# Strassen's algorithm for the output product of a fused attention and gated-layer chain, with its weight tiles and late sources arranged anew

## The chip, the cores and the metric

One core of a Trainium2 chip. The metric is the device time of one execution in microseconds; runs of this kernel differ by a few tenths of a microsecond.

## The reference, cut to what matters

```python
# attention (not touched): p attends k, v; q attends the result
x = attn_out.transpose(0, 2, 1, 3).reshape(B * S, H * D)   # 4608 x 512
# first layer (not touched): w_in 512 x 2048, w_out 2048 x 512
h = x @ w_in
x = (h * sigmoid(h)) @ w_out                               # 4608 x 512
# second layer: w1, w2 512 x 1024, w3 1024 x 1024, w_out 1024 x 512
a = x @ w1
b = x @ w2
h = a * b @ w3
return h @ w_out                                           # 4608 x 512
```

All in fp32.

## The kernel before

Each fp32 operand of a large matmul is split into a high part (rounded to the format of TensorE's fast fp32 mode) and a low part (the rest), and three matmuls add high x high, low x high and high x low. The high part is a ScalarE copy, the low part a subtraction on VectorE or GpSimd (`split_hi` L82, `split_lo` L91, `mm3` L98 to L100). Matmuls take 128x128 stationary tiles.

*First stage* (up to about 865 us). Attention and the first layer run over `items`, (batch, half, 128 rows of d_ff): `ps_h` products, a gate (`sg`, `gg`), its parts (`gh`, `gl`), `ps_x` products. The rows x are stored to `x2_d` in DRAM. In the last batches, `prepare_second` (L950) prepares the second layer's weights between these items. It decodes w1, w2, w3 and w_out; it multiplies w3 by w_out (`product`, L1012), so that one 1024x512 matrix remains, in eight tiles of 128 rows, whose split parts go to `w34_d`; and for half of w1 and w2 it forms the seven left factors of Strassen's algorithm (`left_factors` L935, parts `w12s`), which go to `w12_d`. The steps of `left_factors` wait in a list, `later`, from which `some(2)` takes two at a time. The decoded sources of the other half are stored to `late_d`. Six items before the stage's end (`prep_end`, L1064) the pool `early` opens, the first 768 tokens (`x2r`), two units of left factors and the first two weight tiles are loaded, and `first_right_factors` (L1113) makes the right factors of these tokens (tiles `xcb..`, `xct..`).

*Second stage*. The 4608 tokens are six groups g of 768 (GT), d_ff of the second layer four pairs mp of 128-row tiles: 24 items (g, mp). `emit_ab` (L1280) computes a = x w1 and b = x w2 of an item, one in each pass over x = 0, 1, by Strassen's algorithm in Winograd's form: seven products of 6 matmuls with 384 moving columns (W) in four PSUM banks `b1` to `b4`, in the order a11 b11, s1 t1, s2 t2, a22 t4, a12 b21, s3 t3, s4 b22, with sums on VectorE (L1286) and copies on ScalarE between them. Its weights are a unit (1.8 MB) in four buffers, `wunits`; `load_unit` (L1162) refills a buffer when its pass is over. In the second pass, `gate` (L1301) multiplies a by b and splits the result into `abh`, `abl`. `emit_o` (L1360), called for the item before within the first pass, is the plain output product: six tiles of 128 tokens, for each six matmuls of 512 columns (two weight tiles `w34`, three parts) into one of four banks `ps_o`. In the first item of a group ScalarE copies the result to the accumulator `oacc[t]`, in the others VectorE adds it (L1373), and the last stores it.

While the first two items run, `last_left_factors` (L1180) makes the left factors of w1's and w2's other half: for each of four pieces it loads two sources from `late_d` into `zl`, makes sums and parts (each step behind one product of `emit_ab`, three at a time) and writes each part to `w12_d`; low parts are all on GpSimd. Units 4 and 5 may be loaded only when 22 and 44 of these steps are out. Within each group, the rows of the next group are loaded (`load_x2`, L1088, after the first item), `right_sums` (L1139, GpSimd) forms its sums, and in the last item's second pass `right_factors` (L1153) splits them, alternately with GpSimd and VectorE for the low parts.

All DMAs of the second stage are issued by SP's queue in order. Each engine executes its own instructions in a fixed order, which a planner sets when the program is built: it orders by a modelled time, and among ready instructions by the order in the source. Matmuls of `ps_o` and `ps_ab` therefore stand mixed in the trace, and a load can stand ahead of its place in the source.

## Time and profile before

| | |
|---|---|
| median of 3 runs | 1457.34 us (1457.23 to 1457.74) |
| profiled execution | 1457.94 us, of which the span (first to last instruction) 1455.70 us |
| TensorE matmuls / weight loads busy | 1388.5 us (95%) / 1298.9 us (89%), 8540 each |
| VectorE, ScalarE, GpSimd busy | 959.4 us (66%), 685.3 us (47%), 684.9 us (47%) |
| mean granted TensorE clock | 0.986 of full speed |

Times are us from the span's start. PE is TensorE, PEld its weight loads, DVE VectorE, ACT ScalarE, POOL GpSimd, SP the engine that issues most DMAs. Matmuls are pipelined, so the distance of two starts, and not the length of a row, is what one costs. A line number can be that of a helper (L82, L91, L98 to L100); the tile names tell what is computed. "<-" in a group is output from inputs; behind a wait it names what ended it.

### The profile page before, as it was taken

How to read it: one execution, taken by the hardware profiler on the slowest of the kernel's cores; microseconds unless marked ns; L12 is line 12 of the kernel's file. 1: busy time of each engine (PE TensorE's matmuls, PEld its weight loads, DVE VectorE, ACT ScalarE, POOL GpSimd, SP SyncE). 2: the span in 40 equal slices, each digit the busy share in tenths (PEclk: the TensorE clock that was granted, in tenths of full speed). 3: DMA queues.
4: the chain of work that ended last, by engine and by line, in shares of the span. 5: the costliest groups of instructions: out<-in, count | busy, mean ns of one | idle time of the engine just before them, and what ended most of it. 6: DMA issues, size and time to landing. Idle time of an engine off the chain costs nothing.

```text
span 1455.7 us, 24332 instructions
## 1 busy us (share of the span) xinstructions
PE 1388.5 (95%) x8540; PEld 1298.9 (89%) x8540; DVE 959.4 (66%) x1812; ACT 685.3 (47%) x1531; POOL 684.9 (47%) x666
## 2 busy tenths in 40 slices
PE   7799899999999999999999999599999999999998
PEld 5588799899999999999998998499999989899897
DVE  5897866569776588667499746365574565645646
ACT  6866555555665556654465544132233322332321
POOL 3768755856879657686676525222040120310100
PEclk9899999999999999999999999799999999999999
DMA  8597545845567444562567578946464464554521
GB/s 317 187 308 251 167 142 169 262 135 152 160 199 227 145 134 141 174 178 79 184 218 237 197 289 298 359 153 239 152 226 165 158 233 184 197 211 152 196 102 44
DMA packets 147802, 281.04 MB, mean 193 GB/s; under 512 B 14560, under 2 KB 98784, under 8 KB 141536
## 3 DMA queue, kind: packets, MB, share of 16 engines
q1 hardware_dynamic: 137184, 266.91, 54.9%
q10 hardware_dynamic: 10496, 12.59, 2.4%
q8 instruction: 67, 1.10, 0.3%
q14 instruction: 55, 0.45, 0.1%
HBM read 213.12 MB, written 66.32 MB: 192 GB/s over the span
## 4 chain that ended last, share of the span: by engine, by line
PE 72%; DVE 9%; DMA 7%; issue 5%; ACT 4%; POOL 2%; SPq 1%; ACTq 0%; DVEq 0%; POOLq 0%
PE ps_ab L1272 22%; PE ps_x L98 6%; PE ps_x L99 6%; PE ps_x L100 6%; PE ps_o L98 5%; PE ps_o L99 5%; PE ps_o L100 5%; PE ps_h L98 3%; PE ps_h L100 3%; PE ps_h L99 3%; DMA m_d<-ms 1%; DMA unit<-w_d 1%; DVE gg L846 1%; DMA mr<-m_d 1%; PE ps_w L98 1%
## 5 line engine op out<-in xcount | busy, mean ns | idle before, releaser
L98 PE MATMUL ps_x<-gh,wo 128*128 128x288 f32 x1024 | 301.1, 297 | 2.2 <-DVE xs L883 0.6
L99 PE MATMUL ps_x<-gh,wo 128*128 128x288 f32 x1024 | 300.2, 296 | 0.0
L100 PE MATMUL ps_x<-gl,wo 128*128 128x288 f32 x1024 | 288.9, 297 | 1.5 <-POOL gl L91 1.4
L91 POOL TENSOR_TENSOR gl<-gg,gh 128x288 fp32r<-128x288 f32 x256 | 227.6, 891 | 102.0 <-ACT gh L82 83.0
L1272 PE MATMUL ps_ab<-xct,unit 128*128 128x384 f32 x1152 | 231.1, 340 | 4.0 <-DVE r L1286 4.0
L1272 PEld LDWEIGHTS ps_ab<-xct,unit 128*128 128x128 f32 x1152 | 206.4, 190 | 9.7 <-DVE r L1286 6.6
L98 PEld LDWEIGHTS ps_x<-gh,wo 128*128 128x128 f32 x1024 | 192.4, 188 | 5.6 <-DVE xs L883 2.0
L1272 PE MATMUL ps_ab<-xcb,unit 128*128 128x384 f32 x864 | 179.3, 340 | 16.1 <-DMA unit<-w_d 16.1
L99 PEld LDWEIGHTS ps_x<-gh,wo 128*128 128x128 f32 x1024 | 192.6, 188 | 2.1 <-issue 1.2
L82 ACT ACTIVATE gh<-gg 128x288 fp32r<-128x288 f32 x256 | 112.7, 443 | 167.7 <-DVE gg L846 160.1
L100 PEld LDWEIGHTS ps_x<-gl,wo 128*128 128x128 f32 x1024 | 188.1, 189 | 3.7 <-POOL gl L91 2.8
L91 POOL TENSOR_TENSOR mq<-mr,mq 128x256 fp32r<-128x256 f32 x168 | 137.4, 818 | 109.7 <-DVE mq L86 53.8
L846 DVE SCALAR_TENSOR_TENSOR gg<-sg,ps_h 128x288 f32<-128x288 f32 x256 | 114.5, 447 | 104.6 <-ACT sg L841 51.7
L91 POOL TENSOR_TENSOR xcb<-x2r,xcb 128x768 fp32r<-128x768 f32 x15 | 32.5, 2183 | 308.7 <-ACT xcb L82 308.7
L98 PE MATMUL ps_h<-a,mq 128*128 128x288 f32 x512 | 156.1, 305 | 20.4 <-DVE gg L846 16.2
L1272 PEld LDWEIGHTS ps_ab<-xcb,unit 128*128 128x128 f32 x864 | 155.6, 190 | 22.2 <-issue 11.8
L99 PE MATMUL ps_h<-a,mq 128*128 128x288 f32 x512 | 152.1, 297 | 0.0
L100 PE MATMUL ps_h<-a,mq 128*128 128x288 f32 x512 | 151.7, 296 | 0.0
L841 ACT ACTIVATE sg<-ps_h 128x288 f32<-128x288 f32 x256 | 103.4, 405 | 82.3 <-PE ps_h L100 52.0
L1286 DVE TENSOR_TENSOR r<-p,ps_ab 128x384 f32<-128x384 f32 x96 | 52.8, 550 | 129.7 <-PE ps_ab L1272 129.6
L82 ACT ACTIVATE p<-ps_ab 128x384 f32<-128x384 f32 x96 | 47.1, 492 | 176.0 <-PE ps_ab L1272 99.9
L98 PEld LDWEIGHTS ps_h<-a,mq 128*128 128x128 f32 x512 | 96.7, 189 | 28.6 <-DVE gg L846 21.3
(182 smaller groups left out, 2874.6 us busy)
## 6 DMA issues: line engine op xcount, KB each, us to landing
unit<-w_d SPq DMA_DIRECT2D x48, 1792.0 KB, 6.7
mr<-m_d SPq DMA_DIRECT2D x144, 128.0 KB, 2.6
raw<-in_moe_w_dram SPq DMA_DIRECT2D x32, 512.0 KB, 4.1
wz<-wi_d SPq DMA_DIRECT2D x48, 256.0 KB, 3.8
m_d<-ms SPq DMA_DIRECT2D x96, 128.0 KB, 3.0
x_d<-xs SPq DMA_DIRECT2D x20, 576.0 KB, 3.6
raw<-in_moe_w_out_dram SPq DMA_DIRECT2D x22, 512.0 KB, 4.1
out_dram<-ob SPq DMA_DIRECT2D x36, 256.0 KB, 4.9
```

The costliest lines, as they stand in the source:

```text
L82: A.activation(out=dst, in_=src, func=ACTF.Copy, scale=mul)
L91: (eng or V).tensor_tensor(out=lo, in0=src, in1=hi.bitcast(F32), op=ALU.subtract)
L98: T.matmul(out=dst, lhsT=wh, rhs=xh, start=start, stop=False)
L99: T.matmul(out=dst, lhsT=wl, rhs=xh, start=False, stop=False)
L100: return T.matmul(out=dst, lhsT=wh, rhs=xl, start=False, stop=stop)
L841: ins = A.activation(out=sg, in_=ps, func=ACTF.Tanh, scale=0.5)
L846: ins = V.scalar_tensor_tensor(out=gg, in0=sg, scalar=1.0, in1=ps, op0=ALU.add, op1=ALU.mult)
L1272: T.matmul(out=bank, lhsT=w[:, kt, LEFT[left], wp], rhs=xt[:, kt, xp], start=first and (kt, n) == (0, 0), stop=last and (kt, n) == (1, 2), ...
L1286: V.tensor_tensor(out=dst, in0=p, in1=q, op=op)
```

## The change

The output product too is computed by Strassen's algorithm. For each item the gated 768 tokens x 256 features are a 2x2 block matrix (a11 .. a22) with four sums s1 .. s4, all split into `lf` parts in `left_part`; the pair of weight tiles is a 2x2 block matrix (b11 .. b22) with four differences t1 .. t4. Seven products of nine matmuls (256 columns, three token tiles, three parts) go to chains of PSUM tiles of two banks, two of them at a time (`ps_o`, bufs 2, before 4 of one bank); the partial sums after each product are added to five accumulators of 768 columns in SBUF. After a group's last item GpSimd (VectorE at the very end) adds accumulator 3 to 5 and subtracts 4 from it. The seven steps stand as single steps between the products of the next item's `emit_ab`.

The weight factors of the first two pairs are made in `prepare_second` and stored in split form (`w34f_d`), by ScalarE's queue; the other two pairs stay whole in `w34_d` and are made in the second stage (`last_right_steps`), behind the late left factors. The sources of the first two late pieces are loaded at `prep_end`, into a ring of four `tmp` slots that also holds all sums. The late left factors go through one buffer with four writes for each piece, and part of their low parts go to VectorE. There are three unit buffers instead of four. `load_x2` moves behind a group's third item.

```diff
@@ prepare_second
+    def right_steps(z, sums, part):
+        b11, b12, b21, b22 = z
+        t1, t2, t3, t4 = (sums[:, i] for i in range(4))
...
+        return [
+            lambda: part("b11", b11), lambda: sub_(t1, b12, b11), lambda: part("t1", t1),
+            lambda: sub_(t2, b22, t1), lambda: part("t2", t2), lambda: sub_(t3, b22, b12),
+            lambda: part("b22", b22), lambda: sub_(t4, t2, b21), lambda: part("t3", t3),
+            lambda: part("b21", b21), lambda: part("t4", t4),
+        ]
...
-                    t = dp.tile([128, 2, 512], F32R, tag="w34s", name="w34s")
-                    split(t[:, 0], t[:, 1], ps_w)
-                    move(out=w34_d[i], in_=t)
+                    t = dp.tile([128, 512], F32, tag="w34s", name="w34s", bufs=5)
+                    act_copy(t, ps_w)
+                    z34[i] = t
+                    if i >= KM2 // 2:
+                        store(out=w34_d[i], in_=t, age=0)
+                    elif i > 1:
...
+                        def part(name, src):
+                            t = dp.tile([128, 2, 256], F32R, tag="w12s", name="w12s", bufs=4)
+                            split(t[:, 0], t[:, 1], src)
+                            store(out=w34f_d[mp][:, SECOND[name]], in_=t, age=0)
+
+                        later.extend(right_steps(z, sums, part))
...
-                        some(2)
+                        some(3)
@@ second stage, weights
+    def spare_tmp(k, n):
+        t = early.tile([128, 1024], F32, tag="tmp", name="tmp", bufs=4)
+        return t[:, 0:k * n].rearrange("p (k n) -> p k n", k=k)
...
+    def last_right_steps(mp):
+        w34[mp] = mid.tile([128, 7, 2, 256], F32R, tag=f"w34_{mp}", name=f"w34_{mp}")
+        t = spare_tmp(2, 512)
+        for y, m in enumerate(pair(mp)):
+            move(out=t[:, y], in_=w34_d[m])
+        sums = spare_tmp(4, 256)
+        def part(name, src):
+            d = w34[mp][:, SECOND[name]]
+            split(d[:, 0], d[:, 1], src, eng=G if name[0] == "b" else V)
...
@@ last_left_factors
-        z = load(0)
         for n in range(4):
             x, kt = divmod(n, 2)
-            sums = low.tile([128, 4, 256], F32, tag="suml", name="suml")
+            sums = spare_tmp(4, 256)
+            both = mid.tile([128, 2, 7, 2, 128], F32R, tag="w34_3", name="w12l")
             def part(j, src):
-                t = low.tile([128, 2, 2, 128], F32R, tag="w12s", name="w12s", bufs=7)
-                split(t[:, :, 0], t[:, :, 1], src.rearrange("p (j n) -> p j n", j=2), eng=G)
-                move(out=w12_d[:, 2:4, x, kt, j], in_=t)
+                t = both[:, :, j]
+                split(t[:, :, 0], t[:, :, 1], src.rearrange("p (j n) -> p j n", j=2), eng=G if j < 4 else V)
+                for js in {3: [slice(0, 4)], 6: [slice(4, 7)]}.get(j, []):
+                    for half in range(2):
+                        move(out=w12_d[:, 2 + half, x, kt, js], in_=both[:, half, js])
...
@@ at prep_end
-            for _ in range(2):
-                room_unit(early)
-                load_unit()
+            room_unit(early)
+            load_unit()
             load_w34(early, 0)
+            for n in range(2):
+                load_zl(n)
@@ emit_ab
+        before = o_steps(i - 1) if i else []
+        at_once = () if final else (2, 4, 6, 7, 8, 10, 11)
...
+        def left_part(name, src, eng=None):
...
+                c = mid.tile([128, 2, W], F32R, tag=f"lf{name}", name="lf")
+            split(c[:, 0], c[:, 1], src, eng=eng)
+            parts[name] = c
...
             def step():
+                if place[0] in at_once and before:
+                    before.pop(0)()
+                place[0] += 1
...
-                gate(m1, 0)
+                a11 = gate(0, 0)
+                left_part("a11", a11)
...
+                a12 = gate(1, 0)
+                a22 = gate(1, 1)
+                left_part("a12", a12, G)
+                left_part("a22", a22, G)
...
+                a21 = gate(0, 1)
+                s12, s34 = (spare_tmp(2, W) for _ in range(2))
+                add(s12[:, 0], a21, a22)
+                left_part("s1", s12[:, 0])
+                add(s12[:, 1], s12[:, 0], a11, ALU.subtract)
+                left_part("s2", s12[:, 1])
+                add(s34[:, 1], a12, s12[:, 1], ALU.subtract)
+                left_part("s4", s34[:, 1], G)
+                add(s34[:, 0], a11, a21, ALU.subtract)
+                left_part("s3", s34[:, 0], G)
@@ o_steps, in place of emit_o
+        def sum_up(k, ps):
+            if k not in oacc:
+                oacc[k] = low.tile([128, 3, 256], F32, tag=f"o{k}", name="ob")
+                act_copy(oacc[k], ps)
+            else:
+                V.tensor_tensor(out=oacc[k], in0=oacc[k], in1=ps, op=ALU.add)
...
+        def run(chain_, left, right, fresh, done, k):
+            if fresh:
+                banks[chain_] = ps_o.tile([128, 1024], F32, tag="o", name="ps_o")[:, 0:768]
+            ps = banks[chain_].rearrange("p (t n) -> p t n", t=3)
+            for t in range(3):
+                l = parts[left][:, :, 128 * t:128 * t + 128]
+                w = w34[mp][:, SECOND[right]]
+                for n, (lp, wp) in enumerate(((0, 0), (1, 0), (0, 1))):
+                    T.matmul(
+                        out=ps[:, t], lhsT=l[:, lp], rhs=w[:, wp], start=fresh and t != 1 and n == 0,
+                        stop=done and t != 0 and n == 2, skip_group_check=True,
+                    )
+            sum_up(k, ps)
...
+            run("a", "a11", "b11", True, False, 1)
+            run("b", "s1", "t1", True, False, 5)  
+            run("a", "s2", "t2", False, False, 2) 
+            run("b", "s4", "b22", False, True, 2) 
+            run("a", "s3", "t3", False, True, 3)  
+            run("c", "a12", "b21", True, True, 1) 
+            run("d", "a22", "t4", True, True, 4)  
@@ the loop over items2
-        if mp == 0 and g + 1 < NG:
-            with tc.issue_after(behind["xs"]):
-                load_x2(g + 1)
+        if mp == MP - 2 and g + 1 < NG:
+            load_x2(g + 1)
```

## Rows read from the trace of the kernel before

**Rows 1.** The page: parts 1, 2 and 5 (count, busy, mean ns)
```profile
PE 1388.5 (95%) x8540; PEld 1298.9 (89%) x8540; DVE 959.4 (66%) x1812; ACT 685.3 (47%) x1531; POOL 684.9 (47%) x666
...
PEclk9899999999999999999999999799999999999999
...
L1272 PEld LDWEIGHTS ps_ab<-xct,unit 128*128 128x128 f32 x1152 | 206.4, 190 | 9.7 <-DVE r L1286 6.6
```

**Rows 2.** Windows: length, busy us of PE, PEld, DVE, ACT, POOL; clock, DMA
```profile
977.67:1351.60 373.93, 370.72 (x1921) 343.47 (x1921) 219.13 (x373) 110.81 (x212) 63.83 (x33) 1.00 0.53 192
977.67:1001.05 23.38, 22.58 (x118) 20.68 (x118) 18.03 (x30) 5.89 (x12) 9.96 (x6) 1.00 0.82 286
1024.40:1047.80 23.40, 23.40 (x125) 21.85 (x124) 13.47 (x26) 5.34 (x11) 0.00 (x0) 1.00 0.43 161
```

**Rows 3.** Waits of PE, 900 to 960 us, then 960 to 1450 us
```profile
PE ps_ab L1272 <- DMA unit<-w_d: 16.1, 2, 11.3
...
PE ps_ab L1272 <- DVE r L1286: 4.0, 5, 0.8
```

**Rows 4.** Timeline of PE, start and length; 10 such matmuls lie between
```profile
1199.79 0.40 PE L98 MATMUL ps_o<-w,abh 128*128 128x512 f32 x1
...
1202.36 0.40 PE L100 MATMUL ps_o<-w,abh 128*128 128x512 f32 x1
```

**Rows 5.** Timeline of PE; 14 matmuls like the first lie between
```profile
157.81 0.28 PE L98 MATMUL ps_o<-v,e 128*128 128x256 f32 x1
...
159.59 0.30 PE L98 MATMUL ps_h<-a,mq 128*128 128x288 f32 x1
```

**Rows 6.** Groups by line, DVE and POOL, 960 to 1440 us
```profile
L1373 DVE TENSOR_TENSOR ob<-ob,ps_o 128x512 f32<-128x512 f32 x94 | 60.6, 684 | 58.6 <-PE ps_o L100 58.4
...
L1286 DVE TENSOR_TENSOR r<-p,ps_ab 128x384 f32<-128x384 f32 x82 | 45.1, 550 | 98.7 <-PE ps_ab L1272 98.7
...
L91 POOL TENSOR_TENSOR xcb<-x2r,xcb 128x768 fp32r<-128x768 f32 x15 | 32.5, 2183 | 308.7 <-ACT xcb L82 308.7
...
L1111 POOL TENSOR_TENSOR xt<-x2r 128x768 f32<-128x768 f32 x4 | 7.4, 1845 | 38.7 <-DMA x2r<-x_d 28.6 <-DVE ob L1373 10.0
```

**Rows 7.** Timelines of POOL (first row) and DVE, 1068 to 1077 us
```profile
1068.79 4.67 POOL L91 TENSOR_TENSOR xcb<-x2r,xcb 128x768 fp32r<-128x768 f32 x2
...
1070.04 1.73 DVE L1303 TENSOR_TENSOR r<-r 128x384 f32<-128x384 f32 x1
1071.69 0.54 DVE L1286 TENSOR_TENSOR r<-p,ps_ab 128x384 f32<-128x384 f32 x1
...
1075.60 0.55 DVE L1286 TENSOR_TENSOR r<-r,p 128x384 f32<-128x384 f32 x1
1076.07 0.55 DVE L1303 TENSOR_TENSOR r<-r 128x384 f32<-128x384 f32 x1
```

**Rows 8.** Chain of waits, 840 to 975 us; last, timeline of SP
```profile
864.72 2.67 PE ps_ab L1272 x14
...
929.63 3.39 DMA w_d<-w12s
933.13 9.86 DMA unit<-w_d
...
869.58 0.80 SPq L115 DMA_DIRECT2D zl<-late_d  x2
```

**Rows 9.** Groups by line, POOL, 860 to 932 us
```profile
L91 POOL TENSOR_TENSOR w12s<-suml,w12s 128x256 fp32r<-128x256 f32 x16 | 14.1, 900 | 11.0 <-ACT w12s L82 11.0
```

**Rows 10.** Window; DVE, 740 to 846 us; waits of PE, 680 to 862
```profile
740.00:840.00 100.00, 98.32 (x618) 90.92 (x617) 85.45 (x143) 58.07 (x134) 63.85 (x62) 1.00 0.68 222
...
L91 DVE TENSOR_TENSOR w12s<-sums,w12s 128x256 fp32r<-128x256 f32 x16 | 11.5, 720 | 0.0
...
PE ps_w L98 <- DVE w34s L91: 1.7, 2, 1.4
```

**Rows 11.** Timeline of PE, the last matmul
```profile
1451.56 0.40 PE L100 MATMUL ps_o<-w,ab 128*128 128x512 f32 x1
```

More of the change, by code (lines that the diff above doesn't have):

```diff
@@ L1173, in load_w34 @@
     def load_w34(pool, mp):
-        for m in pair(mp):
-            w34[m] = pool.tile([128, 2, 512], F32R, name=f"w34_{m}")
-            move(out=w34[m], in_=w34_d[m])
-    left_steps = [0]
-    def last_left_factors():
-        def load(n):
-            t = low.tile([128, 2, 512], F32, tag="zl", name="zl", bufs=2)
-            for y in range(2):
-                move(out=t[:, y], in_=late_d[2 * n + y])
-            return [t[:, y] for y in range(2)]
-        z = load(0)
+        w34[mp] = pool.tile([128, 7, 2, 256], F32R, tag=f"w34_{mp}", name=f"w34_{mp}")
@@ new lines, in load_w34 @@
+        move(out=w34[mp], in_=w34f_d[mp])
+    def last_right_steps(mp):
[7 more added lines that the diff above has]
+            split(d[:, 0], d[:, 1], src, eng=G if name[0] == "b" else V)
+        z = [t[:, y, 256 * c:256 * c + 256] for y in range(2) for c in range(2)]
+        for step in right_steps(z, sums, part):
+            step()
+            yield
@@ L1198, in last_left_factors @@
-            nz = load(n + 1) if n < 3 else None
-            for step in left_factors(z, sums, part):
+                t = both[:, :, j]
[3 more added lines that the diff above has]
+                        move(out=w12_d[:, 2 + half, x, kt, js], in_=both[:, half, js])
+            z = zl.pop(n)
+            for step in left_factors([z[:, y] for y in range(2)], sums, part):
@@ L1253, in attention_swiglu_chain @@
     mid = ctx.enter_context(tc.tile_pool(name="mid", bufs=1))
-    ps_o = ctx.enter_context(tc.tile_pool(name="ps_o", bufs=4, space=PSUM))
+    ps_o = ctx.enter_context(tc.tile_pool(name="ps_o", bufs=2, space=PSUM))
     ps_ab = ctx.enter_context(tc.tile_pool(name="ps_ab", bufs=1, space=PSUM))
     top = ctx.enter_context(tc.tile_pool(name="top", bufs=1))
+    w34[1] = top.tile([128, 7, 2, 256], F32R, tag="w34_1", name="w34_1")
     for _ in range(2):
@@ L1259, in attention_swiglu_chain @@
         load_unit()
-    for mp in range(1, MP):
-        load_w34(mid, mp)
+    move(out=w34[1], in_=w34f_d[1])
     items2 = [(g, mp) for g in range(NG) for mp in range(MP)]
-    abt = {}
-    oacc = {}
     def product(bank, w, g, left, right, first, last):
@@ L1276, in product, with first_side @@
                 )
-    side = [last_left_factors()]
+    def first_side():
+        yield from last_left_factors()
+        for mp in range(2, MP):
+            yield from last_right_steps(mp)
+    side = [first_side()]
+    ORDER = ("a11", "s1", "s2", "s4", "s3", "a12", "a22")
+    sums = {}
     def emit_ab(i):
@@ L1356, in emit_ab @@
                 load_unit()
[L1357 to L1376 removed]
+        while before:
+            before.pop(0)()
```

109 lines of the change are left out of this document (65 added, 44 removed).

## The prediction

> **What bounds the kernel now.** I read the page's busy shares and clock first [rows 1]: TensorE is busy 95% of the span at nearly full granted clock, and the one dent late in the span (0.7 of full speed, in the 26th of 40 slices) lies just behind the start of the second stage, where the `ps_ab` products begin. Then that stage by windows [rows 2]: from 977.67 us on, four groups of four items (an item is one `emit_ab` with the output product that belongs to it) take 373.93 us, 93.48 us a group, with 92.7 us of TensorE, 54.8 us of VectorE and 16.0 us of GpSimd in each. Then TensorE's waits [rows 3]: after 960 us it waits 4.0 us in five pieces, one at each change of group, and between 900 and 960 us 16.1 us for `unit` loads alone. So time can go in two places: the number and width of TensorE's matmuls over 24 items, and the hole at the start. VectorE and GpSimd matter as far as TensorE waits for them.
>
> **Output product, the main term.** Before, an item has 6 token tiles x 2 halves x 3 parts = 36 matmuls of 512 columns. After, it has 7 products x 3 token tiles x 3 parts = 63 of 256 columns. The durations in rows include latency, so I take distances of starts. 512 columns: 11 matmuls from 1199.79 to 1202.36 us, 0.2336 us each [rows 4]. 256 columns: this kernel has a dense run of fifteen, 157.81 to 159.59 us, 0.1187 us each [rows 5]. An item pays 36 x 0.2336 = 8.41 us before and 63 x 0.1187 = 7.48 us after, 0.93 us less; I round down to 0.9 for other spots of the trace with a little less than 0.2336, and 24 x 0.9 = **-21.6 us**. The 84 `ps_ab` matmuls of an item stay.
>
> By the two rows a matmul costs 0.449 ns a column plus about 4 ns, so the 27 further weight loads of an item lie hidden behind matmuls. The Trainium skill, "TensorE: Matmul & The Clock Gate", section "The mechanism", says against this change that a weight load overlaps matmuls in flight only where its row group differs, and here all loads fill all rows. By that rule, and 107 ns for a load of 128 columns by the same page's section "LDWEIGHTS" (an estimate), an item would go from 36 x (230 + 107) ns = 12.1 us to 63 x (115 + 107) ns = 14.0 us. The distances in rows 4 and 5 don't agree with it, and the sum goes by them.
>
> **VectorE in an item.** Removed: six adds of 512 columns into `oacc` and one of four low parts (three of the new seven low parts stay on VectorE, four go to GpSimd). Added: seven adds of 768 columns from PSUM and four sums of 384 columns (`s12`, `s34`). One add takes 0.55 us at 384 columns and 0.684 at 512 [rows 6], so about 0.95 at 768; in a full queue starts lie 0.47 us apart at 384 columns [rows 7], 0.08 under the duration, so 0.87 us at 768. After: 8 adds from `ps_ab` x 0.47 + 7 x 0.87 + 13 operations from SBUF (2 on `r2`, 4 gates, 3 low parts, 4 sums) x 0.47 = 3.8 + 6.1 + 6.1 = 16.0 us. The same count gives 12.1 us for before, and a window of one item has 13.5 us [rows 2], so I expect 16 to 17.5 us beside 22.2 us of TensorE (23.1 less 0.9, where 23.1 is a group of 93.48 without its stall of 1, over four). In a group's second item five of the seven adds are ScalarE copies.
>
> The unknown is GpSimd. While it runs, VectorE's operations with both inputs in SBUF take 1.73 us instead of 0.55, and those with an input in PSUM keep 0.54 [rows 7]. GpSimd now makes four low parts of 384 columns in every item; between 0.90 us for 256 columns [rows 9] and 2.18 for 768 [rows 6] that is 1.1 us each, 4.4 in all. If each blocks VectorE for its own length, that is 17.5 + 4.4 = 21.9 us, just under 22.2. The Trainium skill, "SBUF — State Buffer", section "SBUF: two separate sides", says that of the two engines the loser of the shared port waits out the other's whole instruction; by that rule 21.9 us is the most. The 1.73 us of the row on all 13 operations would make it more (a rival below). For items inside a group I take 0 us, near the row without GpSimd, since GpSimd runs a fifth of the time; the ends are 0 and +2 us an item.
>
> **Change of group**, five times. Here GpSimd also makes low parts of `xcb` and `xct` (2.2 us each), and VectorE is at 18.0 us of 23.4 [rows 2]. The 16.0 - 12.1 = 3.9 us of new work make it 22 us of 22.2, and 4.4 us of GpSimd come on top. Ends: 0 us, as TensorE has nine-matmul pieces of the output product to put between, and 26.4 - 22.2 = +4.2 us. I take **+1.5 us x 5 = +7.5 us**, nearer the lower end because TensorE waits only 4.0 / 5 = 0.8 us there today. `load_x2` is issued behind a group's third item instead of its first, so behind four more unit loads on SP's queue. I count 0: the sums on `x2r` need four GpSimd operations of 1.85 us [rows 6], 7.4 us, and an item remains for them. Without that cover each group would wait for most of those 7.4 us.
>
> **Start of the second stage.** From 864.72 us [rows 8] to the last matmul's end, 1451.96 us [rows 11], are 587.2 us. 24 x 23.1 = 554.9 us of it is work, 4 us the changes of group, about 2 us `ps_x` matmuls that run in between; the rest, 26 us, is the hole: 16.1 us of waits for `unit`, smaller ones, and the low clock behind them. The chain shows its parts [rows 8]: low parts, a write of `w_d` of 3.39 us, a unit load of 9.86 us, landed at 943 us. The third item's second unit is due at 864.7 + 2 + 14.8 + 23.1 + 11.5 = 916 us. The 28 low parts, 0.90 us each on GpSimd [rows 9], start late because `zl` is first loaded at 869.58 us [rows 8].
> After, the first two sources lie in SBUF by then, and the chain starts at 866 us. Four halves follow each other through one buffer (`both`): each has 4 low parts on GpSimd (3.6 us) and 3 low parts and 4 sums on VectorE (7 x 0.72 = 5.0 us by the row of the same shape, rows 10), which exclude each other by rows 7: 9 us; then 3.4 us of writes. 4 x 12.4 = 50 us, to 916 us; a unit load of 9.9 us makes it 926 us. Due is 915 us. So 11 us of wait and 2 us of low clock are left of 26: **-13 us**. Ends: -26 if the halves interleave with the main line's gaps, and 0, because 22 steps for the last two weight tiles (`last_right_steps`, 14 low parts and 8 sums, some 17 us of VectorE and GpSimd) now lie in the same stretch.
>
> **First stage.** Eight low parts of 512 columns (0.68 us each as in rows 6) go; 14 low parts and 8 subtractions of 512 columns in pairs or of 256, at 0.72 us each [rows 10], come: 15.8 - 5.4 = +10 us of VectorE. It is busy 85.45 of 100 us from 740 to 840 us [rows 10], so 10 us more just fit. What doesn't fit delays the end of `prepare_second`, for which the load of `x2r` waits. Ends 0 and +10; I take +3. The bank `ps_w` is then read by a ScalarE copy alone, and TensorE's 1.7 us wait for VectorE's read of it [rows 10] goes. Together **+1.3 us**. The bytes loaded at the end of the stage stay about the same: one unit and two small weight tiles go, one wide tile and four `zl` loads come.
>
> **Tail.** Between the last matmul's end and the span's end lie 3.7 us [rows 11]: an add of 0.68 us and a store. After: an add of 0.95, a subtraction of 0.9, the store: **+1.2 us**.
>
> **Sum**, on the profiled execution's own time: -21.6 + 7.5 - 13 + 1.3 + 1.2 = -24.6 us. Its span is 1455.70 us and 2.24 lie around it (1457.94 us), 0.6 us above the runs' median of 1457.34. Predicted: 1457.34 - 24.6 = **1433 us**.
>
> **Rivals.**
> 1. *The start gains nothing.* VectorE gets some 30 further small operations in a stretch of 70 us, and the four slots of `tmp` are shared by sources, sums and the items' own sums. Against: the chain starts before the first item instead of in it. 1433 + 13 = 1446 us.
> 2. *All hides.* The start's wait goes and the changes of group stay as they are: 1433 - 13 - 7.5 = 1412 us. For it: TensorE never waits inside a group now.
> 3. *VectorE becomes the bound (slower).* If the 13 operations from SBUF take 1.1 us instead of 0.47 on average, an item has 3.8 + 6.1 + 14.3 = 24.2 us of VectorE, 2.0 over TensorE: 24 x 2.0 = 48 us, less the 7.5 already counted: 1473 us. From 0.95 us on average VectorE is above TensorE's 22.2, from 1.02 the gain per item is gone. Against: 4.4 of 22 us of GpSimd can't meet most of the 13.
> 4. *The weight loads show (slower).* With every load in series at the 0.19 us that its row gives [rows 1], an item pays 63 x 0.305 = 19.2 us against 36 x 0.420 = 15.1, +4.1 us instead of -0.9: 1433 + 120 = 1553 us. Against: rows 4 and 5.
>
> **Chances.** Forecast, 1424 to 1442 us: 0.54. Rival 1, 1442 to 1453: 0.18. Rival 2, 1408 to 1424: 0.12. Rival 3, 1453 to 1480: 0.15. Rival 4: 0.01. The range 1417 to 1455 us leaves out half of rival 2, nearly all of rival 3 and rival 4. Within 0.2% (2.9 us, about what a measurement can tell from no change) lies the edge of rival 3: 0.03. Faster: 0.54 + 0.18 + 0.12 - 0.01 = 0.83; slower: 0.14.
>
> **What will show it.** `ps_o` matmuls 0.119 us apart in pieces of nine; a group's window of 89 to 91 us instead of 93.5 (93 and more, with waits of `ps_ab` for VectorE inside items, is rival 3); VectorE at 16 to 18 us in a group's third item; waits for `unit` of about 11 us after 900 us; the first `ps_ab` matmul still at 864 to 868 us. A group's window above 93.5 us, or a hole of 26 us at the start, makes the forecast wrong.

## The result and the profile after

Median of 4 runs 1477.78 us (1474.48 to 1479.67) against 1457.54 us for the kernel before on the same chip: ratio 1.0135, 95% interval 1.0121 to 1.0148. The change makes the kernel 20 us slower; 1433 us were forecast. The profiled execution has a span of 1477.3 us, 21.6 us more than before.

I divide both spans at starts that the timelines show: the 4600th matmul (the same work in both up to there; over all executions of this study it starts between 699 and 706 us), the first `ps_ab` matmul, the first one of item 4, that of item 23, and the end. All differences below are of these profiled executions; the forecast column sorts the prediction's terms into the same stretches (-0.9 us an item with its own stretch). The last column is the best kernel of the study (e15, below). Two executions of the same code differ too: up to item 22 e6 (below) has this kernel's code, and its items 0 to 3 take 116.6 us, not 118.7.

| stretch, us | before | after | difference | forecast | e15 |
|---|---|---|---|---|---|
| first 4600 matmuls | 701.7 | 702.8 | +1.1 | 0 | 701.5 |
| to the first `ps_ab` | 163.0 | 169.4 | +6.4 | +1.3 | 164.6 |
| items 0 to 3 | 110.9 | 118.7 | +7.8 | -16.6 | 101.4 |
| items 4 to 22 | 444.3 | 441.9 | -2.4 | -9.6 | 434.1 |
| item 23 and the end | 35.8 | 44.4 | +8.6 | +0.3 | 44.6 |

First the page after, against [rows 1]: fewer busy microseconds of TensorE in more and narrower matmuls, 159 us more of VectorE, 120 us more of GpSimd.

```profile
PE 1385.1 (94%) x9188; PEld 1328.6 (90%) x9188; DVE 1118.5 (76%) x1958; ACT 733.9 (50%) x1625; POOL 804.6 (54%) x766
...
PEclk9899999999999999999999998799999999999998
...
L1454 DVE TENSOR_TENSOR ob<-ob,ps_o 128x768 f32<-128x768 f32 x138 | 130.2, 948 | 41.1 <-PE ps_o L1469 25.3
```

The main term came out. PE's timeline after (start, length): eight `ps_o` matmuls from 1050.50 to 1051.46 us are 0.120 us apart, where the one of 512 columns took 0.2336 [rows 4].

```profile
1050.50 1.12 PE L1469 MATMUL ps_o<-w,lf 128*128 128x256 f32 x8
1051.46 0.34 PE L1325 MATMUL ps_ab<-xcb,unit 128*128 128x384 f32 x1
```

The windows that answer to [rows 2] (length; busy PE, PEld, DVE, ACT, POOL; clock, DMA share, GB/s): four groups, a third item, an item at a change of group. Four groups take 371.3 us, 92.8 each on average (91.5 to 94.5), against 93.5; 91.4 was forecast. The third item has its 22.2 us; the one at the change has 27.3, with VectorE busy for 24.39 of them and a mean granted clock of 0.94.

```profile
991.00:1362.30 371.30, 361.41 (x2344) 356.71 (x2344) 314.25 (x436) 137.84 (x255) 147.70 (x104) 1.00 0.54 192
1040.10:1062.30 22.20, 22.20 (x149) 22.20 (x148) 19.28 (x31) 6.87 (x15) 4.27 (x4) 1.00 0.45 166
1083.40:1110.70 27.30, 24.70 (x149) 23.75 (x148) 24.39 (x33) 6.89 (x15) 12.66 (x9) 0.94 0.59 207
```

PE's waits after, 860 to 960 us and then 960 to 1450 (total, times, longest): the 16.1 us of waits for `unit` [rows 3] are gone, and 25.3 us of waits for `lf` and `ob` stand there. Later there are 11.3 us instead of 4.0.

```profile
PE ps_o L1469 <- ACT lf L82: 15.6, 2, 14.5
PE ps_o L1469 <- DVE ob L1454: 4.9, 3, 3.6
PE ps_o L1469 <- DVE lf L91: 4.8, 2, 4.5
...
PE ps_ab L1325 <- DVE r L1348: 3.8, 6, 1.4
PE ps_o L1469 <- DVE ob L1454: 3.8, 5, 1.0
PE ps_o L1469 <- DVE lf L91: 2.6, 7, 0.8
PE ps_ab L1325 <- ACT r L82: 1.1, 1, 1.1
```

Windows of the first stage after, which [rows 10] answers to: from 780 to 820 us TensorE, full before, has 17.8 and 17.2 of 20 us at a clock of 0.91. VectorE is at 18 to 19 of 20 until 840 us, then at 4: the new work is bunched. Whether it is also too much, e2 tests.

```profile
780.00:800.00 20.00, 17.76 (x104) 16.20 (x103) 18.81 (x30) 12.91 (x32) 10.58 (x10) 0.91 0.62 201
800.00:820.00 20.00, 17.17 (x99) 15.27 (x97) 18.06 (x30) 10.09 (x25) 8.94 (x8) 0.91 0.76 247
820.00:840.00 20.00, 20.00 (x126) 18.47 (x125) 18.26 (x33) 12.75 (x31) 13.23 (x13) 1.00 0.60 199
840.00:860.00 20.00, 20.00 (x136) 19.04 (x135) 4.00 (x11) 6.07 (x14) 8.44 (x11) 1.00 0.40 130
```

The start of the second stage, by ScalarE's timeline after. The first copies into the late factors' buffer (`w12l`) stand at 896 us, 21 us after the first sum of their sources (874.7 us). The next two sets wait for writes of that buffer. The `lf` copies on which the output product waits 14.5 us follow at 926.70; the sums that they copy stand on VectorE behind low parts that wait for the same set (last two rows, VectorE's timeline).

```profile
896.14 2.25 ACT L82 ACTIVATE w12l<-tmp 128x256 fp32r<-128x256 f32 x7
898.29 1.34 ACT L82 ACTIVATE lf<-r 128x384 fp32r<-128x384 f32 x3
...
911.93 2.26 ACT L82 ACTIVATE w12l<-tmp 128x256 fp32r<-128x256 f32 x7 [2.83 <-DMA w_d<-w12l]
922.29 2.25 ACT L82 ACTIVATE w12l<-tmp 128x256 fp32r<-128x256 f32 x7 [8.10 <-DMA w_d<-w12l]
926.70 1.46 ACT L82 ACTIVATE lf<-tmp 128x384 fp32r<-128x384 f32 x3 [2.16 <-DVE tmp L1348]
...
923.97 2.23 DVE L91 TENSOR_TENSOR w12l<-tmp,w12l 128x256 fp32r<-128x256 f32 x3 [5.31 <-ACT w12l L82]
926.12 1.01 DVE L1348 TENSOR_TENSOR tmp<-r 128x384 f32<-128x384 f32 x2
```

Why 896 us: the pool `mid`, where the buffer lies, takes the memory of the first stage's last `xs`. SP's timeline after shows the store of that tile issued at 886.35 us, behind loads that wait; it landed at 894.9. Before it was issued at 870.48 (last row). In this execution the first copy shows no wait of its own, since it stands behind a copy of `r` that began at 895.75; that the store holds it is shown by e2 (below), where ScalarE's copies wait for that store by name, and by e5.

```profile
874.85 6.92 SPq L115 DMA_DIRECT2D x2r<-x_d  x3
881.82 3.47 SPq L115 DMA_DIRECT2D tmp<-late_d  x2
885.34 0.90 SPq L115 DMA_DIRECT2D x2r<-x_d  x1
886.35 1.62 SPq L115 DMA_DIRECT2D x_d<-xs  x1
...
870.48 0.36 SPq L115 DMA_DIRECT2D x_d<-xs  x1
```

The end, in PE's timeline after: 90 `ps_o` matmuls in 18.8 us (10.7 at 0.119 each), which wait until VectorE's adds free one of the two pairs of PSUM banks, and from 1462 us on run at a mean clock of 0.72.

```profile
1455.31 1.33 PE L1469 MATMUL ps_o<-w,lf 128*128 128x256 f32 x9 [1.05 <-DVE ob L1454]
1457.98 1.29 PE L1469 MATMUL ps_o<-w,lf 128*128 128x256 f32 x9 [1.35 <-DVE ob L1454]
1460.57 0.55 PE L1469 MATMUL ps_o<-w,lf 128*128 128x256 f32 x1 [1.29 <-DVE ob L1454]
1462.12 8.94 PE L1469 MATMUL ps_o<-w,lf 128*128 128x256 f32 x53 [1.00 <-DVE lf L91]
```

### The profile page after: what moved, and what is told of

Same layout as the page of the kernel before. It is cut to its first block, busy times and chain, and to the rows that moved or that the text cites. A ratio compares the mean times of both kernels' runs of the same rounds, so it can differ in the third digit from the quotient of the medians.

```text
span 1477.3 us, 26034 instructions
## 1 busy us (share of the span) xinstructions
PE 1385.1 (94%) x9188; PEld 1328.6 (90%) x9188; DVE 1118.5 (76%) x1958; ACT 733.9 (50%) x1625; POOL 804.6 (54%) x766
## 4 chain that ended last, share of the span: by engine, by line
PE 51%; DVE 18%; issue 4%; DMA 4%; ACT 3%; SPq 0%; ACTq 0%; POOL 0%; DVEq 0%; POOLq 0%
PE ps_ab L1325 18%; PE ps_o L1469 9%; PE ps_x L98 4%; PE ps_x L99 4%; PE ps_x L100 4%; DVE ob L1454 2%; DVE tmp L1348 2%; PE ps_h L98 2%; PE ps_h L100 2%; PE ps_h L99 2%; DVE r L1348 2%; DVE r L1358 1%; DVE lf L91 1%; DVE gg L847 1%; DMA kq<-in_k_dram 1%
## 5 line engine op out<-in xcount | busy, mean ns | idle before, releaser
L1469 PE MATMUL ps_o<-w,lf 128*128 128x256 f32 x1512 | 220.5, 291 | 36.3 <-ACT lf L82 15.6
L1469 PEld LDWEIGHTS ps_o<-w,lf 128*128 128x128 f32 x1512 | 207.6, 197 | 42.3 <-ACT lf L82 24.1
L1325 PE MATMUL ps_ab<-xct,unit 128*128 128x384 f32 x1152 | 225.8, 339 | 3.8 <-DVE r L1348 3.8
L1325 PEld LDWEIGHTS ps_ab<-xct,unit 128*128 128x128 f32 x1152 | 200.6, 189 | 6.6 <-DVE r L1348 6.6
L847 DVE SCALAR_TENSOR_TENSOR gg<-sg,ps_h 128x288 f32<-128x288 f32 x256 | 114.6, 448 | 113.5 <-ACT sg L842 57.2
L91 POOL TENSOR_TENSOR lf<-r,lf 128x384 fp32r<-128x384 f32 x48 | 51.9, 1085 | 228.3 <-ACT lf L82 157.4
L1454 DVE TENSOR_TENSOR ob<-ob,ps_o 128x768 f32<-128x768 f32 x138 | 130.2, 948 | 41.1 <-PE ps_o L1469 25.3
L1325 PEld LDWEIGHTS ps_ab<-xcb,unit 128*128 128x128 f32 x864 | 150.9, 190 | 2.2 <-ACT r L82 1.3
```

The source lines that it names most:

```text
L91: (eng or V).tensor_tensor(out=lo, in0=src, in1=hi.bitcast(F32), op=ALU.subtract)
L847: ins = V.scalar_tensor_tensor(out=gg, in0=sg, scalar=1.0, in1=ps, op0=ALU.add, op1=ALU.mult)
L1325: T.matmul(out=bank, lhsT=w[:, kt, LEFT[left], wp], rhs=xt[:, kt, xp], start=first and (kt, n) == (0, 0), stop=last and (kt, n) == (1, 2), ...
L1454: V.tensor_tensor(out=oacc[k], in0=oacc[k], in1=ps, op=ALU.add)
L1469: T.matmul(out=ps[:, t], lhsT=l[:, lp], rhs=w[:, wp], start=fresh and t != 1 and n == 0, stop=done and t != 0 and n == 2, skip_group_check ...
```

## The experiments

Ratios are to the kernel before, run beside each; over all these runs it takes 1454.6 to 1463.4 us, so its runs differ by more than a few tenths. "Off" is against the changed kernel's 1477.8 us. e1 to e3 and e5 to e7 are the changed kernel with one edit. Stretches are as in the table above, of one execution each.

**e1: two buffers for the late left factors.**

```diff
-            both = mid.tile([128, 2, 7, 2, 128], F32R, tag="w34_3", name="w12l")
+            both = mid.tile([128, 2, 7, 2, 128], F32R, tag=f"w34_{2 + n % 2}", name="w12l")
```

> The changed kernel, with the late left factors going through two buffers in turn (the rooms of the third and the fourth pair's weights) instead of one. Theory: at the start of the second stage the lf copies of the first item stand on ScalarE behind copies into the one buffer, which wait for its write to DRAM; with two buffers the 14.5 us wait of ps_o for lf goes, items 0 to 3 take 105 us instead of 118.8, the time falls by 10 to 14 us to about 1465. Rival: VectorE is full in that stretch anyway (16 sums, 12 low parts, and 22 steps for the weights); then the wait moves to VectorE and the time falls by under 3 us.

1473.69 us, ratio 1.0105 (1.0081 to 1.013), 4 us off, though this interval meets that of the changed kernel. Items 0 to 3 fall from 118.7 to 110.6 us, the longest wait for `lf` from 14.5 to 4.4, and items 4 to 22 of that execution are 4.7 us longer. The wait for the buffer's writes was real, but gave little of the whole: both buffers lie in `mid`, and the first copies still start at 895 us.

**e2: the weights' preparation two steps at a time.**

```diff
-                        some(3)
+                        some(2)
```

> The changed kernel, with two steps at a time taken from the list in the first stage as before, instead of three. Theory: three at a time bunch the new low parts and differences between 780 and 820 us, where VectorE is 18.8 and 18.1 of 20 us busy and TensorE loses 5 us, while from 840 to 860 us VectorE is only 4.0 of 20 us busy; with two the first ps_ab matmul comes at 866 us instead of 872, and the time falls by 5 us. Rival: it is the amount of VectorE work and not its place; then the first ps_ab matmul stays at 871 to 874 us or comes later, since the stage waits for the last of the steps.

1468.82 us, ratio 1.0076 (1.006 to 1.0093), 9 us off, more than expected. The stretch to the first `ps_ab` falls from 169.4 to 163.4 us, 0.4 above before. So the first stage's +6.4 us is bunching: the operations themselves fit beside TensorE. All runs here agree: with three steps at a time (seven kernels) the stretch takes 167.0 to 169.5 us, with two (eight kernels) 163.4 to 165.2. Items 0 to 3 take 114.9 us; the store of `xs` lands at 887.3 us here. ScalarE's timeline of e2 also shows what the late factors' buffer waits for:

```profile
887.39 2.26 ACT L82 ACTIVATE w12l<-tmp 128x256 fp32r<-128x256 f32 x7 [1.38 <-DMA x_d<-xs]
```

**e3: short adds.** It leaves out 744 of the 768 columns of every sum into `oacc` after the first copy.

```diff
-                V.tensor_tensor(out=oacc[k], in0=oacc[k], in1=ps, op=ALU.add)
+                V.tensor_tensor(out=oacc[k][:, :, 0:8], in0=oacc[k][:, :, 0:8], in1=ps[:, :, 0:8], op=ALU.add)
```

> The changed kernel, with the adds into the accumulators cut to 24 of 768 columns (the rest of the sum is left out): the same order of waits, but about 0.15 us of VectorE instead of 0.87 for each of the 138 adds. Theory (VectorE is too full in the first two items of a group): the four groups from item 4 on take 89 to 90 us instead of 92.8, and the tail from item 23 on loses 4 us; the span falls by 20 us or so. Rival (GpSimd's port blocks VectorE, or the two banks of ps_o are too few, whatever the adds cost): groups stay at 92 us or more.

1454.51 us in a single run. Items 4 to 22 take 432.2 us (441.9), with 91.0 us a group, between the theory's 89 to 90 and the rival's 92; item 23 with the end 37.7 (44.4), items 0 to 3 114.6 (118.7). With VectorE relieved of some 0.8 us for each of the adds, two of the four losses go: groups and end hang on VectorE's adds. As these also free the banks, the run doesn't tell VectorE's queue from the number of banks.

**e4: the kernel before with its late sources loaded in the first stage.**

```diff
-        z = load(0)
+        z = zl.pop(0)
...
+            for n in range(2):
+                load_zl(n)
```

The last two lines stand at `prep_end`; `zl` moves to `early`.

> The kernel before, with only one part of the change: the sources of the first two late left factors are loaded at the end of the first stage (the two zl slots move to the pool that opens there). Theory: the chain of late left factors starts 10 us earlier, the hole of 26 us before 945 us shrinks by about 10, time 1445 to 1450 us. Rival: the chain is paced by GpSimd and by writes behind each other, the time stays at 1457 within 3 us.

1457.47 us, ratio 0.9996 (0.9985 to 1.0007): nothing. PE still waits 17.3 us for `unit` between 900 and 960 us (before 16.1). The first low parts do start at 868.9 us (before 880.0), but what follows is paced by later loads and writes. The prediction's reason for a gain at the start, an earlier source, is worth nothing alone.

**e5: the late factors' buffer in other memory.** It changes places with `w34_1`, and the fourth pair's weight tile, which shares its memory, moves with it.

```diff
-            both = mid.tile([128, 2, 7, 2, 128], F32R, tag="w34_3", name="w12l")
+            both = top.tile([128, 2, 7, 2, 128], F32R, tag="w34_3", name="w12l")
...
-        w34[mp] = mid.tile([128, 7, 2, 256], F32R, tag=f"w34_{mp}", name=f"w34_{mp}")
+        w34[mp] = (top if mp == 3 else mid).tile([128, 7, 2, 256], F32R, tag=f"w34_{mp}", name=f"w34_{mp}")
...
-    w34[1] = top.tile([128, 7, 2, 256], F32R, tag="w34_1", name="w34_1")
+    w34[1] = mid.tile([128, 7, 2, 256], F32R, tag="w34_1", name="w34_1")
```

> The buffer of the late left factors (w12l) changes places with the weight tile w34_1: it lies in the pool top, whose memory is free once the last ps_h product is read, and w34_1 lies in mid. In the changed kernel the first ScalarE copies into w12l stand at 896.1 us, although their sources were on chip before 874.7 us, where the first sum of them was made; the memory of the buffer held the last xs, whose store was issued at 886.4 us and landed at 893.8 us. Theory (the chain starts late because its buffer waits for that store): first copies at 875 to 882 us, the waits of ps_o for lf behind them shrink, items 0 to 3 take 118.8 - 10 = 109 us or less, total -8 to -15 us against 1477.8. Rival (the engines have too much to do there, wherever the late work starts): the copies start earlier, but items 0 to 3 stay at 116 us or more and the total is within 3 us.

1463.71 us, ratio 1.0044 (1.0029 to 1.006), 14 us off. ScalarE's timeline of e5: the copies start 20 us earlier, though the store of `xs` lands as late (895.1 us; in the changed kernel 894.9, the 893.8 above being e1's).

```profile
876.31 1.32 ACT L82 ACTIVATE w12l<-tmp 128x256 fp32r<-128x256 f32 x4
```

Items 0 to 3 fall to 108.4 us: the memory's old owner cost some 10 us there.

**e6: the last item's pieces spread.**

```diff
-        at_once = () if final else (2, 4, 6, 7, 8, 10, 11)
+        at_once = (2, 4, 6, 7) if final else (2, 4, 6, 7, 8, 10, 11)
```

> In the last item four of the seven pieces of the output product of the item before stand between its products, as in all other items, and three behind them; in the changed kernel all seven stand behind, and ten more follow. Theory (at the end every piece waits for VectorE to add the one two before it, behind gates and sums that GpSimd slows): the last item to the last matmul falls from 37.9 to 33 us, the total by 4 to 6 us. Rival (the time is set by the chain from the last ps_ab product to the last lf part, and the pieces only lie in its gaps): TensorE waits for lf instead of for ob, 36.5 us or more, total within 1.5 us.

1475.25 us, ratio 1.0119 (1.0094 to 1.0144). The last item keeps its 38.0 us, and its waits are for `ob` as before (3.4 us), not for `lf`. Neither theory was put to the test: the planner had put pieces between the products already, and the order at the end stayed.

**e7: the low parts of `lf` on VectorE.**

```diff
-                left_part("a12", a12, G)
+                left_part("a12", a12)
```

and so for a22, s4, s3.

> The four low parts of an item that the changed kernel gives to GpSimd (a12, a22, s4, s3) are made by VectorE. Theory (GpSimd's operations slow VectorE's SBUF operations by about as much as they save: r 797 and tmp 1013 to 1369 ns on average against 547 to 563 free): VectorE gets 4 x 0.47 = 1.9 us more to do in an item and loses about 3.2 us of slowing, so its busy time over four groups falls or stays, items inside a group stay at 22.2 us and groups at 91 to 93 us; total -5 to +1 us. Rival (VectorE's number of operations is what counts): VectorE 26 us in the items at a change of group, groups of 95 us, total +8 us or more.

1463.90 us, ratio 1.0043 (1.0026 to 1.0059), 14 us off, more than the theory had. In the profile items 4 to 22 give 3.2 us, items 0 to 3 give 5.0, item 23 1.5; the rest, 5 us, lies ahead of the first `ps_ab`, where the code is the same. VectorE is busy 321 us in the four groups, 314 in the changed kernel, and the groups take 367.9 us instead of 371.4. More work for VectorE and less time: the rival is out.

**e8: e2, e5, e6 and a second buffer together.** The buffer's line differs from e5's:

```diff
+            both = (mid if n % 2 else top).tile([128, 2, 7, 2, 128], F32R, tag=f"w34_{3 - n % 2}", name="w12l")
```

> The edits of e2 (two steps of the weights' preparation at a time), e5 (buffer elsewhere) and e6 (last item spread) together, and a second buffer for the late left factors as in e1. If the terms lie in different stretches and add up: e2 gave -9, e1 -4; with -10 for e5 and -5 for e6 the time is 1478 - 28 = 1450 us, below the kernel before (1457.5). If they share one cause (VectorE's load), what one gives another takes: 1462 us or more.

1460.50 us, ratio 1.002 (1.0004 to 1.0037). They don't add up to 1450, a sum that counted on 5 us of e6 which had not come: items 0 to 3 stay at 109.7 us. At 930 us eleven copies of the last weight tiles now stand ahead of `lf`, and PE waits 8.6 us.

**e9: the steps of those tiles taken one at a time.**

```diff
-            steps = 3 if i < 2 else 1
...
+                for _ in range(3 if i < 2 and left_steps[0] < 56 else 1):
```

> As e8, and the steps for the last two weight tiles (last_right_steps) are taken one at a time behind each product from the moment the late left factors are out, not three at a time. In e8 eleven ScalarE copies of these tiles (w<-tmp) stand at 930 us in front of the lf copies of the second item, behind sources that landed at 931 us, and ps_o waits 8.6 us for lf at 938 us; they are not needed before 953 us. Theory (parts of the item that runs stand behind work that isn't due in the engines' fixed order): that wait goes, items 0 to 3 take 102 us instead of 109.7, total -6 to -8 us against e8 (1460.5), 1453 us. Rival (the engines are full there, and the work only comes later): items 0 to 3 at 107 us or more, total within 2 us of e8.

1461.53 us, ratio 1.0022 (1.0001 to 1.0043): no gain. The order on ScalarE stayed (eleven copies, then `lf`), with a wait of 8.5 us, so this run speaks for neither side. Where the step stands in the source did not decide here; the planner orders by its modelled time.

**e10: e9 and e7.**

> As e9, and the four low parts of an item that GpSimd makes are made by VectorE, as in e7. Theory (contention): e7 took 3 us off the groups from item 4 on, 5 off the first four items and 1.5 off the end; most of it again, so 5 to 9 us below e9. Rival (in e9 VectorE is at 18 to 20 of 20 us in parts of the first 100 us of the stage and at the changes of group, so 1.9 us more in an item costs as much as it saves): within 2 us of e9 or above.

1457.00 us, ratio 0.9999 (0.9983 to 1.0016), 4.5 us below e9, with intervals that overlap; items 0 to 3 106.6 us (108.0), item 23 with the end 42.9 (44.6), items 4 to 22 as in e9 (436.8 against 437.1). Less than the theory had.

**e11: e10, and the low parts of `xcb`, `xct` all on VectorE.**

```diff
-            right_part(g, name, sums_of[g][name], V if n % 2 else G)
+            right_part(g, name, sums_of[g][name], V)
```

> As e10, and the low parts of the next group's right factors (xcb, xct), of which GpSimd makes four of seven, are all made by VectorE. Theory (at a change of group TensorE waits because VectorE's SBUF operations take 1.3 to 1.8 us instead of 0.55 beside GpSimd's, and the waits trip the clock): GpSimd's 4 x 2.1 us there go, VectorE gets 4 x 0.87 = 3.5 us, and the item at a change falls from 24 to 27 us to 23 to 25; about -1.5 us a group, -7 us against e10. Rival (VectorE's own work is the bound at a change: 24 of 25 us): +2 us a group, +10 us.

1451.48 us, ratio 0.9958 (0.9943 to 0.9973), the first that beats the kernel before. Items 4 to 22 take 432.8 us; the item at a change of group falls to 20 to 23 us, and the next one rises from 24 to 26.6.

**e12: e11, and the steps of the last weight tiles ordered behind the second item's last `lf`.**

```diff
+        while "lfl" not in behind:
+            yield
         for step in right_steps(z, sums, part):
-            step()
+            with hold("lfh", "lfl"):
+                step()
...
+            if i == 1:
+                behind["lfh"], behind["lfl"] = hi.ins, lo.ins
```

> As e11, and the 22 steps for the last two weight tiles are held, by an explicit order, behind the low and high copies of the second item's last lf part. In e11 eleven ScalarE copies of these tiles stand ahead of four lf copies from 927.5 us on, wait there for a write, and the first product of ps_o waits 8.2 us for lf. Theory (the loss is the order: work that isn't due, and whose data are late, stands ahead of work that TensorE waits for): the wait at 928 us falls to 2 us or less, items 0 to 3 take 107.2 - 8 = 99 us, total 1451.5 - 8 = 1444 us. Rival (load: the same operations have to run before the third item's end wherever they stand): the wait comes back at w34_2 or at the loads of the units, items 0 to 3 at 104 us or more, total 1449 us or more.

1447.70 us, ratio 0.9924 (0.9912 to 0.9936). First e11's ScalarE, then e12's PE waits from 860 to 990 us:

```profile
927.51 3.58 ACT L82 ACTIVATE w<-tmp 128x256 fp32r<-128x256 f32 x11 [1.77 <-DMA w_d<-w12l]
...
934.99 0.52 ACT L82 ACTIVATE lf<-tmp 128x384 fp32r<-128x384 f32 x1 [0.39 <-DVE tmp L1348]
```

```profile
PE ps_o L1474 <- ACT lf L1370: 5.0, 2, 2.9
PE ps_o L1474 <- DVE ob L1459: 3.1, 2, 2.1
```

The wait of 8.2 us at this place was the order, and the longest is now 2.9 us, but only 3 us come back (items 0 to 3: 104.2, the rival's number; the total lies between the two). The larger part so speaks for the rival: the operations have to run somewhere in this stretch.

**e13: the changed kernel without GpSimd's low parts of `lf`, `xcb` and `xct`, e7's and e11's edits alone.**

> The changed kernel with all low parts of lf, xcb and xct in the second stage on VectorE, and no other edit: GpSimd keeps the sums on x2r, late left factors and weight steps. Theory (contention on GpSimd's account): e7's -14 us and e11's -5.5 us add, 1459 us, groups from item 4 on at 434 us as in e11 (432.8) against 441.9. Rival (what e11 gained hangs on the other edits): 1464 us or more, groups at 438 us or more.

1461.91 us, ratio 1.0025 (1.0016 to 1.0034), 16 us off, 3 above the theory. Items 4 to 22 take 430.7 us, 3 below it, so the edits need no other. Groups by form, 991 to 1362 us (busy, mean ns), of the changed kernel and then of e13:

```profile
L1358 DVE TENSOR_TENSOR r<-r 128x384 f32<-128x384 f32 x64 | 51.3, 814 | 14.9 <-ACT r L82 14.8
...
L91 POOL TENSOR_TENSOR lf<-r,lf 128x384 fp32r<-128x384 f32 x32 | 34.4, 1078 | 151.6 <-ACT lf L82 94.1 <-PE ps_o L1469 40.8 <-PE ps_ab L1325 15.6
...
L1348 DVE TENSOR_TENSOR tmp<-r 128x384 f32<-128x384 f32 x32 | 31.0, 1007 | 0.1
...
L1348 DVE TENSOR_TENSOR tmp<-r,tmp 128x384 f32<-128x384 f32 x16 | 23.6, 1472 | 0.0
...
L1348 DVE TENSOR_TENSOR r<-r,p 128x384 f32<-128x384 f32 x32 | 21.0, 656 | 0.4
```

```profile
L1358 DVE TENSOR_TENSOR r<-r 128x384 f32<-128x384 f32 x67 | 36.0, 552 | 9.6 <-ACT r L82 9.6
...
L1348 DVE TENSOR_TENSOR r<-r,p 128x384 f32<-128x384 f32 x33 | 23.7, 717 | 0.4
...
L1348 DVE TENSOR_TENSOR tmp<-r 128x384 f32<-128x384 f32 x34 | 23.5, 732 | 0.1
...
L1348 DVE TENSOR_TENSOR tmp<-r,tmp 128x384 f32<-128x384 f32 x16 | 12.1, 755 | 0.0
```

VectorE's gates (L1358) and sums of 384 columns with both inputs in SBUF lose up to half of their time when GpSimd has less to do beside them (40 us of 368, in the changed kernel 148 of 371). Not every group does: the sums `r<-r,p` now meet what GpSimd still has, operations of some 2 us, and rise from 656 to 717 ns. By single operations it is plain: in e13 each of the 29 `r<-r,p` that meet no operation of GpSimd takes 0.55 us, the four that meet one 1.9. Four low parts an item come on top for VectorE, and it still pays.

**e14: e12 without late work.**

```diff
-        yield from last_left_factors()
-        for mp in range(2, MP):
-            yield from last_right_steps(mp)
+        yield from ()
...
+    w34[2], w34[3] = w34[0], w34[1]
...
-    move(out=t, in_=w12_d[:, mp, x])
+    move(out=t, in_=w12_d[:, mp % 2, x])
```

> As e12 without any late work in the second stage: it leaves out the late left factors, the last two weight tiles and their loads and writes; the products take the factors of the first two pairs again in their place. Theory (the late work's operations on VectorE, ScalarE and GpSimd, in whatever order, are what stretches the first items): items 0 to 3 fall from 104.2 to 90 us or less, near the 83 us of their matmuls. Rival (the loads of 12 MB at the start, which fill the DMA engines to 920 us, set it): 98 us or more, with waits for unit or w.

1438.29 us in a single run; items 0 to 3 take 93.7 us, between the theories. PE's timeline of e14 has a wait for a unit in the first item (the granted clock from 880 to 900 us is 0.74):

```profile
885.85 2.26 PE L1328 MATMUL ps_ab<-xcb,unit 128*128 128x384 f32 x6 [9.13 <-DMA unit<-w_d]
```

This wait is e14's own: the changed kernel has none for a unit here and e12 one of 1.0 us. SP's timelines of e14 and then of the changed kernel show where it comes from: in e14 the next two units are issued 7.5 us later, behind the rows `x2r`. What put them there isn't shown. With e12's wait in its place items 0 to 3 would take some 86 us (an estimate, 93.7 less 9.1 and plus 1.0), if nothing else came to wait; that is the theory's side.

```profile
876.87 1.06 SPq L115 DMA_DIRECT2D unit<-w_d  x2
...
869.38 0.80 SPq L115 DMA_DIRECT2D unit<-w_d  x2
```

**e15: e12, and the low parts of the late work on VectorE too.**

```diff
-                split(t[:, :, 0], t[:, :, 1], src.rearrange("p (j n) -> p j n", j=2), eng=G if j < 4 else V)
+                split(t[:, :, 0], t[:, :, 1], src.rearrange("p (j n) -> p j n", j=2), eng=V)
...
-            split(d[:, 0], d[:, 1], src, eng=G if name[0] == "b" else V)
+            split(d[:, 0], d[:, 1], src, eng=V)
```

> As e12, and the low parts of the late left factors and of the last weight tiles, of which GpSimd makes four of seven, are all made by VectorE: 28 + 14 of 0.41 us free. Theory (contention: VectorE's w12l, w and tmp operations of 256 columns take 0.7 to 1.2 us beside GpSimd's, 0.41 free): items 0 to 3 fall by 4 us or more to 100 us, total 1443.5. Rival (VectorE's queue is the path there, busy 16 to 18.3 of 20 us, and 24 more operations of 0.41 us cost 5 to 10 us): items 0 to 3 at 104 us or more, total 1447 us or above.

1444.71 us, ratio 0.9902 (0.9886 to 0.9919), 14 us below the kernel before. Against e12 items 0 to 3 fall by 2.8 us, less than the theory had, and the intervals of the two touch; the rival's loss does not come.

## Why the prediction was wrong, step by step

**Output product.** Right: 0.120 us a matmul, 22.2 us in a third item, weight loads hidden. Rival 4 is out.

**VectorE in an item, and the change of group.** A third item had 19.3 us of VectorE where 16 to 17.5 were expected, and TensorE still never waited in it: that item cost nothing, as forecast. The price fell at the change of group: 4.0 us over 4 x 22.2 in a group, against 1.1 before, so +2.9 us instead of +1.5. The term was mis-sized, inside its ends, and the mechanism was the one named: beside GpSimd VectorE's operations stretch (e13, [rows 7]). The Trainium skill, "SBUF — State Buffer", section "SBUF: two separate sides", has the loser of the port wait for the other's whole instruction; the trace agrees, as with an `xct` low part (timelines of GpSimd and VectorE) that took 1.69 us instead of 0.95 beside a GpSimd operation that ended at 1085.77 us.

```profile
1083.59 2.18 POOL L91 TENSOR_TENSOR xcb<-x2r,xcb 128x768 fp32r<-128x768 f32 x1
...
1084.90 1.69 DVE L91 TENSOR_TENSOR xct<-x2r,xct 128x768 fp32r<-128x768 f32 x1
```

It holds in all of the four groups. Of VectorE's operations of 384 columns with both inputs in SBUF, the 75 that began beside a running GpSimd operation, 0.06 us or more before its end, ended 0.41 to 0.47 us after it; the 26 during which a GpSimd operation began took 0.54 to 0.55 us, as without one. Beyond 0.55 us (0.95 for 768 columns) this cost VectorE 60 us in the four groups, against 17 before, 40 in e7 and 30 in e13. Without GpSimd's low parts items 4 to 22 come out 4 us better than forecast (430.7 against 434.7).

**Start of the second stage.** This step failed, by 24 us of the 46 between forecast and result. "The chain starts at 866 us" did not hold: the sources had landed by 874.7 us, and the buffer's memory was free at 894.9 (e2, e5: some 10 us). Its length was right: from the first copy at 896.1 us to the landing of the last write at 946.9 us are 50.8 us, and 50 were forecast. The overlap was wrong as well: writes of the one buffer held ScalarE, and VectorE behind it (e1, 8 us in items 0 to 3, partly the same), and the late work, which I took to lie beside the items, stood ahead of `lf` in fixed orders, so that the wait for `unit` came back as a wait for `lf` (e8, e12). The forecast of 94.3 us for items 0 to 3 left almost nothing for the late work: e14, without any, takes 93.7, of which 9.1 are its own wait for a unit. In its best form here (e15, 101.4) the late work costs 8 us over e14, or 16 over the estimate without that wait; the changed kernel, which has none of e14's other edits, lies 25 and 33 us over them.

**First stage.** The amount was about right, the place wrong: with two steps at a time it costs 0.4 us in e2 and up to 2.2 in the later kernels, around the forecast +1.3; taken three at a time it cost 6.4. One part of the term failed: the wait for the bank `ps_w` did not go with VectorE's read of it, but is 2.5 us for ScalarE's copy (1.7 before).

**Tail.** Priced as one longer add; most of the cost lies before it. 90 matmuls through two pairs of banks follow VectorE's adds, +6.3 us in item 23 up to the last matmul's start and +2.4 behind that. Shorter adds take 6.7 of 8.6 us away (e3). No complete kernel here mends it (e6, e15).

**Rivals.** Rival 3 had the sign and nearly the time (1473), with the wrong place: from item 4 to 22 no item's VectorE was above TensorE's 22.2 us outside the changes of group, and a change that gave VectorE more to do made the kernel faster (e7, e13). In the first items, where the late work is, VectorE was above it: in item 2 it was busy for 31.5 of 37.1 us. Rival 1 (the start gains nothing) came true and worse, beside it.

What stays open: how the end's 8.6 us divide between the banks and VectorE's queue; what of e7's 14 us lies ahead of the second stage, where its code is unchanged; and through which chain GpSimd's low parts cost TensorE time, since in e7 VectorE loses less to GpSimd (40 us instead of 60) and yet is busier in sum (321 us instead of 314).

## What to carry to other kernels

A step that is moved starts when its buffer's memory is free, not when its sources are there: look up what lies there before and when its last store is issued on its queue. In a fixed order per engine, work without a due date that waits for a DMA holds up the copies behind it; here only an explicit order, not its place in the source, moved it, and of a wait of 8 us that gave back 3. Before low parts go to a second engine, look at what the first engine's operations take while the second one runs, and not at the first one's busy time alone: here taking them all back made VectorE busier and a loss of 20 us into one of 4.

## What was not expected of the hardware

The same waits don't always cost the same. In the items at a change of group at 1083 and at 1269 us of the changed kernel TensorE waits 2.6 us each, in the same four pieces, the longest 1.4. In the second the granted clock stays at 1.00 and the item takes 25.9 us; in the first, after the last and longest piece, it is near the lower of its two levels for 3.3 us, and the item takes 27.3. Windows of the changed kernel, columns as above:

```profile
1098.70:1102.00 3.30, 3.25 (x13) 3.25 (x14) 3.27 (x5) 0.58 (x2) 2.90 (x2) 0.54 0.28 114
...
1269.40:1295.30 25.90, 23.34 (x150) 22.39 (x149) 24.21 (x33) 6.89 (x15) 12.64 (x9) 1.00 0.63 219
```

And the share of VectorE's busy time told little of the bound: 85% in the changed kernel's four groups (314 of 371 us) and 89% in e13's (328 of 368 from 1062 us on), where the groups are shorter.
